# Row scatters of the routing stage spread over three steps instead of one

## The chip, the cores and the metric

The kernel runs on one core of one Trainium2 chip. The metric is the device time in microseconds (us) of one execution. A core has a matrix engine (TensorE, PE in the rows, with its weight loads as PEld), a vector engine (VectorE, DVE), an activation engine (ScalarE, ACT), GpSimd (POOL) and a sync engine (SyncE, SP) whose queue issues most of the transfers. Each engine works through its own instructions in order and waits on semaphores that the others raise. Indirect transfers, in which a list of row numbers says where each row goes, are issued by POOL.

## The reference

Three layers run after one another on 3072 tokens of 384 values (4 batches of 768 steps, 8 heads of 48):

```python
# attention: a gated linear recurrence
state = alpha[:, :, t, :, None] * state + einsum('bhd,bhe->bhde', k[:, :, t], v[:, :, t])
y[:, :, t] = einsum('bhd,bhde->bhe', q[:, :, t], state)
# layer 1: each token goes to the best of 8 experts, and is scaled by its probability
expert_idx = argmax(logits, axis=1)          # logits = normed x @ normed emb / tau
out[mask] = gate_w[mask, None] * (maximum(x[mask] @ w1[e], 0) @ w2[e])
# layer 2: all 4 experts for each token, weighted
out += p[:, e:e+1] * (maximum(x @ w1[e], 0) @ w2[e])
```

## The kernel before, in words

The tokens are cut into 24 units of 128. The first stage (about the first 170 us) is a loop over steps `i` of 0 to 28, a software pipeline written out by hand: `S1(i)` multiplies q and k of unit `i` (PE, line 480) and masks the product (DVE, 485), `S2(i-1)` forms the unit's output and the new state (PE, 516, 525, 537; the state update on DVE at 549 and 550), and `S3(i-2)` turns the output to rows of tokens (PE, 558) and copies them into a row buffer `xb` (ACT, 570). The scans that prepare a group of three units (`prep1`) stand on DVE (434, 446) and two multiplications each (`prep2`) on POOL (459, 460). The weights of layer 1 are split into a high and a low part by ACT (74) and POOL (75), one unit of weights in every second step from step 6 (`split_w`).

Units are routed in groups, `ends = [6, 12, 18, 20, 22, 24]`. When the last unit of a group is through `S3`, `route_a`, `rank`, `route_b` and `route_c` choose the expert, the place and the gate value in the next steps. In step `u1 + 4` (`u1` is the group's end) ACT scales all rows of the group (line 645) and POOL scatters them to DRAM, one indirect DMA of 128 rows of 1536 bytes a unit (line 653). The rows go to the tensor `xs`, sorted by expert. After the step of the third group's scatter, `early_load` (line 666, SP) reads the first 224 rows of the largest window back as `exw`. It waits for the scatters of the first 18 units. PE turns `exw` over in step 25 (686) and starts the first expert on it (702 and 724).

The order on each engine is that of the program text. `scatter(r)` stands ahead of `split_w` in its step before, and behind it after. Each of the row buffers is taken again by `S3` of the unit that comes as many units later as there are buffers, and is free when its scatter has landed.

Of the kernel before, what the change touches and what calls it, by code (L numbers as in the profile page):

```python
# [338 lines left out]
def attention_and_routing(tc, a, small, keep, xs, info_d, wst, wtile, load_w, split_w, psA, ps1):  # L339
# [4 lines left out]
    groups = list(zip([0] + ends[:-1], ends))  # L344
    with ExitStack() as ctx:
# [3 lines left out]
        ew = ctx.enter_context(tc.tile_pool(name="ew", bufs=2))  # L349
        bd = ctx.enter_context(tc.tile_pool(name="bd", bufs=5))  # L350
        wk = ctx.enter_context(tc.tile_pool(name="wk", bufs=2))
        xbp = ctx.enter_context(tc.tile_pool(name="xbp", bufs=10))

        cst = c1.tile([128, 736], F32, name="cst")
        ien = cst[0:112, 0:416].rearrange("p (a w) -> p a w", a=4)
# [45 lines left out]
        def load_in(g, pp, lo=0, hi=2311):  # L401
            if (g, pp) not in tins:
                tins[g, pp] = tin.tile([R, 775 + 1536], F32, tag="tin", name="tin")
            nc.sync.dma_start(out=tins[g, pp][:, lo:hi], in_=a["aqk"][g, pp][:, lo:hi])

        def load_v(g):
            v = vin.tile([128, 3, DM], F32, tag="v", name="v")
            nc.sync.dma_start(out=v, in_=a["v"][g])
            vins[g] = v

        def prefill(e):
            nc.sync.dma_start(
                out=xs[e * NR + LOW:e * NR + W0, :].rearrange("(p j) d -> p j d", j=4),
                in_=pre[0:(W0 - LOW) // 4, :].unsqueeze(1).to_broadcast([(W0 - LOW) // 4, 4, DM]),
            )
# [5 lines left out]
        def prep1(g, pp, c0=0, c1=3, part=2):  # L421
            al = tins[g, pp]
            if c0 == 0 and part != 1:
                mid[g, pp] = [
                    bd.tile([R, 774], F32, tag="G", name="G"), bd.tile([R, 774], F32, tag="bf", name="bf", bufs=6)
                ]
            G, bf = mid[g, pp]
            segs = list(range(2 * c0, 2 * c1, 3)) + [2 * c1]
            pieces = list(zip(segs, segs[1:]))
            if part != 1:  # L430
                nc.vector.memset(c3(dcon, CW)[:, :, 0:1], 1.0)
                for s0, s1 in pieces:
                    lo, hi = CW * s0, CW * s1
                    nc.vector.tensor_tensor_scan(  # L434
                        G[:, lo:hi][:, ::-1], al[:, lo + 1:hi + 1][:, ::-1], dcon[:, 0:hi - lo], 0.0,
                        op0=ALU.mult, op1=ALU.max,
                    )
            if part != 0:
                nc.scalar.activation(
                    out=bcall[:, g, c0:c1, 2 * pp:2 * pp + 2],  # L440
                    in_=c3(G, CW)[:, 2 * c0:2 * c1, 0:1].rearrange("p (c a) o -> p c (a o)", a=2), func=AF.Copy,
                )
                for s0, s1 in pieces:
                    lo, hi = CW * s0, CW * s1
                    nc.vector.reciprocal(c3(dcon, CW)[:, 0:s1 - s0, 0:1], c3(G, CW)[:, s0:s1, 0:1])
                    nc.vector.tensor_tensor_scan(  # L446
                        bf[:, lo:hi], al[:, lo:hi], dcon[:, 0:hi - lo], 0.0, op0=ALU.mult, op1=ALU.max
                    )
# [53 lines left out]
        def flush(q):  # L502
            while q:
                q.pop(0)()
# [68 lines left out]
        state, scat = {}, []  # L573
        last = len(groups) - 2

        def route_a(r):
            u0, u1 = groups[r]
            n, sl = u1 - u0, slice(u0, u1)
            rt = root_p(nc, mk, half, ssq[:, sl], n, 128)
            state[r] = rt, choose(nc, mk, wcon, raws(u0, u1), ohb[:, sl, :], n)  # L580
# [51 lines left out]
        def route_c(r):  # L632
            u0, u1 = groups[r]
            n = u1 - u0
            si, ex = state.pop(r)
            gt = gate(nc, mk, ex, n)
            state[r] = si, gt
# [8 lines left out]
                else:  # L646
                    nc.vector.tensor_scalar(xb, xb, gt[:, j:j + 1], None, op0=ALU.mult)

        def scatter(r):
            u0, u1 = groups[r]  # L650
            si = state.pop(r)[0]
            for j in range(u1 - u0):
                ins = nc.gpsimd.indirect_dma_start(
                    out=xs, out_offset=bass.IndirectOffsetOnAxis(ap=si[:, j:j + 1], axis=0),
                    in_=xbs.pop(u0 + j), in_offset=None, bounds_check=E1 * NR - 1, oob_is_err=False,
                )
                tc.declare_no_dep(ins.ins, group="xs", reason="rows of their own")
                tc.add_to_no_dep_group("xs", ins.ins)
                scat.append(ins)
# [118 lines left out]
        def prep_emb3():  # L778
            pe = mk("pe", 128, 4, 8)
            for p in range(4):  # L780
                nc.tensor.matmul(
                    pe[0:112, p, :], lhsT=embp[:, p].rearrange("e s d -> e (s d)")[:, 0:112],
                    rhs=ident[0:8, 0:8], is_transpose=True, start=(p == 0), stop=True, skip_group_check=True,
                )
            nc.vector.tensor_copy(ien[:, :, 96:104], pe[0:112])
# [33 lines left out]
        for i in range(NU + 5):  # L819
            for g in range(2, NG):  # L820
                if max(0, 3 * g - 8) == i:
                    load_in(g, 0)
                if max(0, 3 * g - 6) == i:
                    load_in(g, 1)
            for g in range(1, NG):
                if 3 * g - 2 == i:
                    load_v(g)
            if 0 < i <= E1:
                prefill(i - 1)
            if 5 <= i < 27 and i % 2:  # L830
                load_w(min((i - 3) // 2, NFB))

            steps = []
            for g in range(1, NG):
                for pp in range(2):
                    at = 3 * g - 4 + pp - (g > 2)
                    if g == 1 and pp == i:
                        steps.append((2, lambda g=g, pp=pp: prep1(g, pp)))
                    if g > 1 and at + 1 == i:
                        steps.append((0, lambda g=g, pp=pp: prep1(g, pp, part=1)))  # L840
                    if g > 1 and at == i:
                        steps.append((1, lambda g=g, pp=pp: prep1(g, pp, part=0)))
            steps = [f for _, f in sorted(steps, key=lambda x: x[0])]
            if steps and i > 1:
                steps.pop(0)()
            if 0 < i < NU:
                S1(i)
            if i == 1:
                prep_emb3()
            if 0 <= i - 2 < NU:  # L850
                S3(i - 2)
            for r, (u0, u1) in enumerate(groups):
                if i == u1 + 2 and r < last:
                    rank(r)
            if 0 <= i - 1 < NU:
                S2(i - 1)
            for r, (u0, u1) in enumerate(groups):
                if i == u1 + (3 if r < last else 2) and r <= last:
                    route_b(r)
                if i == u1 + 1:  # L860
                    flush(sums)
                    route_a(r)
                    if r > last:
                        early_rows()
                    if r >= last:
                        rank(r)
                    if r > last:
                        early_g1(0)
                        early_g1(1)
                        hl0 = early_relu(0)  # L870
                        early_g1(2)
                        early_g1(3)
            for f in steps:
                f()
            for g in range(1, NG):
                for pp in range(2):
                    at = 3 * g - 3 + pp - (g > 2)
                    if at == i:
                        prep2(g, pp, nc.gpsimd, nc.gpsimd)
                    if at + 1 == i:  # L880
                        prep4(g, pp)
            if i == 0:
                fill()
            if i == 2:
                prep_info()
            for r, (u0, u1) in enumerate(groups):
                if i == u1 + 1 and r > last:
                    route_b(r)
                if i == u1 + (4 if r < last else 2 if r == last else 1):
                    route_c(r)  # L890
                    scale(r)
                    if r < last:
                        scatter(r)
                    if r > last:
                        scatter(last)
                        scatter(r)
                        count(r)
                        tail(hl0)
            if 6 <= i < 22 and i % 2 == 0:
                split_w((i - 4) // 2)  # L900
            flush(late)
            flush(sums)
            if i == EARLY_U + 5:
                early_load()
# [389 lines left out]
```

## Time and profile before

| | |
|---|---|
| three timed runs, median (lowest, highest) | 1223.74 us (1221.97, 1224.63) |
| the profiled execution | 1219.32 us |
| its span, first to last instruction | 1217.5 us |
| mean granted TensorE clock | 0.987 |
| PE busy | 1177.6 us, 97% of the span |
| DVE, ACT, POOL busy | 393.9, 326.5, 306.8 us |

The times below are in us from the start of the span. In the page's table of 40 slices PE falls below 9 tenths at its start, in the sixth slice (about 152 to 183 us) and at its end.

### The profile page before, as it was taken

The page shows a single profiled execution, that of the slowest core. Times are in us where ns is not written, and L with a number is a line of the kernel's source. Part 1 is how long each engine was busy: PE and PEld are TensorE (multiplying, and loading weights), DVE is VectorE, ACT ScalarE, POOL GpSimd, SP SyncE. Part 2 cuts the span into 40 slices and gives each one's busy share as a digit, 9 for nine tenths or more (in the row PEclk, how much of TensorE's full clock was granted, in tenths as well). Part 3 has the DMA queues.
Part 4 walks back from the last instruction along what each step waited for, and adds up shares of the span by engine and source line. Part 5 has one row for each costly group of instructions (what it writes and reads, how often), then busy time and mean ns, then how long its engine had stood idle before and what let it go on. Part 6 is the DMA issues. An engine that isn't in the chain of part 4 may idle for free.

```text
span 1217.5 us, 17436 instructions
## 1 busy us (share of the span) xinstructions
PE 1177.6 (97%) x7219; PEld 1078.6 (89%) x7219; DVE 393.9 (32%) x823; ACT 326.5 (27%) x640; POOL 306.8 (25%) x221
## 2 busy tenths in 40 slices
PE   5999979999999999999999999999999999999996
PEld 4788879999999999999999999999999999999996
DVE  8989553222222222222212222222222122222221
ACT  3466534444444311111311111221111131111111
POOL 3567543766666300000400000130000030111111
PEclk9999989999999999999999999999999999999998
DMA  9995125544443300000300000120000010000000
GB/s 236 298 278 174 54 100 172 155 141 140 133 123 121 81 1 1 1 1 1 90 15 1 1 1 1 30 75 1 1 1 1 1 40 1 27 27 26 26 27 29
DMA packets 30032, 79.98 MB, mean 66 GB/s; under 512 B 7352, under 2 KB 11064, under 8 KB 28376
## 3 DMA queue, kind: packets, MB, share of 16 engines
q1 hardware_dynamic: 26104, 69.25, 19.5%
q0 software_dynamic: 3840, 9.54, 2.2%
q8 instruction: 58, 0.95, 0.3%
q14 instruction: 30, 0.25, 0.1%
HBM read 65.21 MB, written 13.57 MB: 65 GB/s over the span
## 4 chain that ended last, share of the span: by engine, by line
PE 87%; DVE 4%; issue 3%; ACT 0%; POOL 0%; DVEq 0%; POOLq 0%; ACTq 0%
PE h L135 14%; PE h L137 13%; PE h L136 13%; PE p L303 11%; PE p L302 11%; PE p L301 10%; PE o L234 3%; PE o L235 3%; PE o L233 3%; PE fin L558 1%; PE y L516 1%; PE A L480 1%; DVE bf L446 1%; DVE G L434 1%; DVE At L485 1%
## 5 line engine op out<-in xcount | busy, mean ns | idle before, releaser
L127 DVE SCALAR_TENSOR_TENSOR hl<-h,hh 128x512 fp32r<-128x512 f32 (+9 forms) x264 | 169.9, 644 | 733.4 <-ACT hh L126 719.0
L126 ACT ACTIVATE hh<-h 128x512 fp32r<-128x512 f32 (+9 forms) x264 | 148.2, 562 | 727.1 <-PE h L137 725.3
L75 POOL TENSOR_TENSOR wu<-wraw,wu 128x768 fp32r<-128x768 f32 x96 | 176.6, 1841 | 643.9 <-ACT wu L74 643.7
L303 PE MATMUL p<-wu,hl 128*128 128x384 f32 x768 | 258.8, 337 | 0.0
L302 PE MATMUL p<-wu,hh 128*128 128x384 f32 x768 | 258.2, 336 | 0.0
L301 PE MATMUL p<-wu,hh 128*128 128x384 f32 x768 | 258.0, 336 | 0.0
L135 PE MATMUL h<-x,wu 128*128 128x512 f32 (+1 forms) x600 | 233.0, 388 | 0.0
L137 PE MATMUL h<-x,wu 128*128 128x512 f32 (+1 forms) x600 | 230.6, 384 | 0.0
L136 PE MATMUL h<-x,wu 128*128 128x512 f32 (+1 forms) x600 | 227.9, 380 | 0.0
L302 PEld LDWEIGHTS p<-wu,hh 128*128 128x128 f32 x768 | 144.3, 188 | 7.4
L301 PEld LDWEIGHTS p<-wu,hh 128*128 128x128 f32 x768 | 144.4, 188 | 7.1
L303 PEld LDWEIGHTS p<-wu,hl 128*128 128x128 f32 x768 | 144.3, 188 | 0.0
L137 PEld LDWEIGHTS h<-x,wu 128*128 128x128 f32 x600 | 112.6, 188 | 26.6
L136 PEld LDWEIGHTS h<-x,wu 128*128 128x128 f32 x600 | 112.8, 188 | 16.1
L135 PEld LDWEIGHTS h<-x,wu 128*128 128x128 f32 x600 | 112.8, 188 | 14.5
L74 ACT ACTIVATE wu<-wraw 128x768 fp32r<-128x768 f32 x96 | 80.4, 840 | 39.6 <-PE p L303 34.1
L314 POOL DMA_INDIRECT out_dram<-acc,toki x24 | 23.4, 975 | 183.4 <-DVE acc L310 178.5
L135 PE MATMUL h<-xh,wu 128*128 128x224 f32 (+7 forms) x192 | 67.4, 351 | 0.3 <-DVE xl L198 0.3
L234 PE MATMUL o<-hl,wu 128*128 128x224 f32 (+7 forms) x192 | 65.6, 341 | 0.1
L233 PE MATMUL o<-hh,wu 128*128 128x224 f32 (+7 forms) x192 | 65.6, 342 | 0.0
L136 PE MATMUL h<-xh,wu 128*128 128x224 f32 (+7 forms) x192 | 65.5, 341 | 0.0
L137 PE MATMUL h<-xl,wu 128*128 128x224 f32 (+7 forms) x192 | 65.5, 341 | 0.0
(164 smaller groups left out, 1086.2 us busy)
## 6 DMA issues: line engine op xcount, KB each, us to landing
wraw<-in_wu_dram SPq DMA_DIRECT2D x96, 384.0 KB, 3.1
tin<-in_aqk_dram SPq DMA_DIRECT2D x14, 1011.1 KB, 11.4
xw<-xs SPq DMA_DIRECT2D x7, 672.0 KB, 6.6
v<-in_v_dram SPq DMA_DIRECT2D x8, 576.0 KB, 10.3
xs<-pre SPq DMA_DIRECT2D x8, 480.0 KB, 11.0
tin<-in_aqk_dram SPq DMA_DIRECT2D x2, 448.0 KB
tin<-in_aqk_dram SPq DMA_DIRECT2D x2, 225.8 KB, 4.4
tin<-in_aqk_dram SPq DMA_DIRECT2D x2, 224.0 KB
```

The costliest lines, as they stand in the source:

```text
L74: nc.scalar.activation(out=t[:, 0], in_=r, func=AF.Copy)
L75: nc.gpsimd.tensor_tensor(out=t[:, 1], in0=r, in1=t[:, 0].bitcast(F32), op=ALU.subtract)
L126: nc.scalar.activation(out=hh[:, 0:n], in_=ps, func=AF.Relu)
L127: nc.vector.scalar_tensor_tensor(out=hl[:, 0:n], in0=ps, scalar=0.0, in1=hh[:, 0:n].bitcast(F32), op0=ALU.max, op1=ALU.subtract)
L135: nc.tensor.matmul(ps, lhsT=w[:, 0, ks], rhs=xh(k), start=(k == 0), stop=False)
L136: nc.tensor.matmul(ps, lhsT=w[:, 1, ks], rhs=xh(k), start=False, stop=False)
L137: nc.tensor.matmul(ps, lhsT=w[:, 0, ks], rhs=xl(k), start=False, stop=(k == KD - 1))
L233: nc.tensor.matmul(o, lhsT=w[:, 0, ds], rhs=hh[:, 0:n], start=(f == 0), stop=False)
L234: nc.tensor.matmul(o, lhsT=w[:, 0, ds], rhs=hl[:, 0:n], start=False, stop=False)
L301: nc.tensor.matmul(o, lhsT=hh[:, js], rhs=w[:, 0, DM:2 * DM], start=(f == 0), stop=False)
L302: nc.tensor.matmul(o, lhsT=hh[:, js], rhs=w[:, 1, DM:2 * DM], start=False, stop=False)
L303: nc.tensor.matmul(o, lhsT=hl[:, js], rhs=w[:, 0, DM:2 * DM], start=False, stop=(f == NFB - 1))
```

## The change

The six scatters of the first and of the second group are issued two in each of three steps (`u1 + 4`, `u1 + 5`, `u1 + 6`), those of the third group three in each of two steps (22 and 23), all behind `split_w`. The fourth to sixth group are as before. The row buffers are 12 instead of 10. No transfer is added or left out.

```diff
-        xbp = ctx.enter_context(tc.tile_pool(name="xbp", bufs=10))
+        xbp = ctx.enter_context(tc.tile_pool(name="xbp", bufs=12))
...
-        def scatter(r):
+        def scatter(r, js=None):
             u0, u1 = groups[r]
-            si = state.pop(r)[0]
-            for j in range(u1 - u0):
+            si = state[r][0]
+            for j in js or range(u1 - u0):
...
-                    if r < last:
+                    if r == last - 1:
                         scatter(r)
...
             if 6 <= i < 22 and i % 2 == 0:
                 split_w((i - 4) // 2)
+
+            for r, (u0, u1) in enumerate(groups[:last - 1]):
+                n = 2 if r < 2 else 3
+                k = i - u1 - 4
+                if 0 <= k * n < u1 - u0:
+                    scatter(r, range(k * n, k * n + n))
```

POOL's instructions in steps 9 to 12, round the scatters of the first group (`xs<-xb,si` is a scatter, `wu<-wraw,wu` the split of weights, `bf` and `G` are `prep2`):

```order
 L459 TENSOR_TENSOR bf<-tin,bf 112x6x128
 L460 TENSOR_TENSOR G<-tin,G 112x6x128
-L653 DMA xs<-xb,si 24576x384 x6
 L75 TENSOR_TENSOR wu<-wraw,wu 128x768
+L653 DMA xs<-xb,si 24576x384 x2
 L459 TENSOR_TENSOR bf<-tin,bf 112x6x128
 L460 TENSOR_TENSOR G<-tin,G 112x6x128
+L653 DMA xs<-xb,si 24576x384 x2
 L459 TENSOR_TENSOR bf<-tin,bf 112x6x128
 L460 TENSOR_TENSOR G<-tin,G 112x6x128
 L75 TENSOR_TENSOR wu<-wraw,wu 128x768
+L653 DMA xs<-xb,si 24576x384 x2
```

The six stand now in three pairs, the first behind the split of weights of its step, and between the pairs stand the `prep2` of the next two steps. The second group moves in the same way in steps 16 to 18.

POOL's instructions in steps 20 to 25, round the third to sixth group (`sq_r<-ssq,half`, line 982 before and 988 after, is the root that opens a group's routing):

```order
 L75 TENSOR_TENSOR wu<-wraw,wu 128x768
-L982 TENSOR_TENSOR sq_r<-ssq,half 128x2
-L653 DMA xs<-xb,si 24576x384 x6
-L982 TENSOR_TENSOR sq_r<-ssq,half 128x2
-L653 DMA xs<-xb,si 24576x384 x2
-L982 TENSOR_TENSOR sq_r<-ssq,half 128x2
+L988 TENSOR_TENSOR sq_r<-ssq,half 128x2
+L653 DMA xs<-xb,si 24576x384 x3
+L988 TENSOR_TENSOR sq_r<-ssq,half 128x2
+L653 DMA xs<-xb,si 24576x384 x5
+L988 TENSOR_TENSOR sq_r<-ssq,half 128x2
 L653 DMA xs<-xb,si 24576x384 x4
```

The fifth group's root stands now between the third and the fourth scatter of the third group. The five behind it are the other three of the third group and the two of the fourth.

## Rows read from the trace of the kernel before

**Rows 1.** The page's chain that ended last, shares by engine.

```profile
PE 87%; DVE 4%; issue 3%; ACT 0%; POOL 0%; DVEq 0%; POOLq 0%; ACTq 0%
```

**Rows 2.** Busy us of PE, PEld, DVE, ACT, POOL in two stretches; clock, DMA share, GB/s.

```profile
90.00:120.00 30.00, 28.79 (x368) 25.11 (x367) 28.42 (x73) 19.88 (x51) 21.22 (x15) 0.90 0.59 182
...
190.00:1217.50 1027.50, 1015.90 (x5344) 937.43 (x5344) 246.40 (x412) 235.48 (x399) 206.17 (x135) 1.00 0.14 42
```

**Rows 3.** POOL's timeline, first and last scatter of three sixes: start, length, engine, instruction.

```profile
81.36 1.21 POOL L653 DMA_INDIRECT xs<-xb,si  x1 [4.73 <-ACT xb L645]
...
87.98 0.97 POOL L653 DMA_INDIRECT xs<-xb,si  x1 [0.30 <-issue]
...
117.05 1.06 POOL L653 DMA_INDIRECT xs<-xb,si  x1 [5.70 <-ACT xb L645]
...
123.53 0.98 POOL L653 DMA_INDIRECT xs<-xb,si  x1 [0.30 <-issue]
...
151.92 1.06 POOL L653 DMA_INDIRECT xs<-xb,si  x1 [7.31 <-ACT xb L645]
...
158.40 0.98 POOL L653 DMA_INDIRECT xs<-xb,si  x1 [0.30 <-issue]
159.39 0.74 POOL L982 TENSOR_TENSOR sq_r<-ssq,half 128x2 f32<-128x2 f32 x1
```

**Rows 4.** DVE's timeline at the first and second six; idle time before and releaser in brackets.

```profile
84.76 1.81 DVE L434 TENSOR_TENSOR_SCAN G<-tin,dcon 112x387 f32<-112x387 f32 x2
90.05 0.37 DVE L549 TENSOR_TENSOR U<-U,S 112x192 f32<-112x192 f32 x1 [3.48 <-PE fin L558]
...
125.73 0.37 DVE L549 TENSOR_TENSOR U<-U,S 112x192 f32<-112x192 f32 x1 [3.47 <-PE A L480]
```

**Rows 5.** PE's timeline: the state product of step 11, first products of steps 18, 19, 21, 22.

```profile
84.09 0.67 PE L537 MATMUL U<-v,kn_s 128*64 128x48 f32 x16
...
121.94 0.49 PE L480 MATMUL A<-bf,G 48*128 48x128 f32 x4
...
130.98 1.16 PE L480 MATMUL A<-bf,G 48*128 48x128 f32 x16
...
140.48 1.16 PE L480 MATMUL A<-bf,G 48*128 48x128 f32 x16
...
145.62 1.16 PE L480 MATMUL A<-bf,G 48*128 48x128 f32 x16
```

**Rows 6.** Timelines of PE, ACT and SP at the third six; DMA view's landing of exw.

```profile
154.19 1.08 PE L525 MATMUL y<-bf,S 48*48 48x128 f32 x16
...
160.56 0.60 ACT L529 ACTIVATE yt<-y 112x512 f32<-112x512 f32 x1 [5.47 <-PE U L537]
...
161.19 0.33 SPq L666 DMA_DIRECT2D exw<-xs  x1
...
exw<-xs SPq DMA_DIRECT2D x1, 336.0 KB, 3.1
...
167.76 0.74 PE L686 MATMUL ext<-ti,exw 112*128 112x112 f32 x6
```

**Rows 7.** A pair's second scatter, ACT beside it; busy us round four scatters of the output.

```profile
172.39 0.97 POOL L653 DMA_INDIRECT xs<-xb,si  x1 [0.30 <-issue]
...
173.58 0.55 ACT L710 ACTIVATE eh<-eh 128x448 fp32r<-128x448 f32 x1 [3.62 <-PE eh L702]
...
1041.00:1047.50 6.50, 6.50 (x34) 5.72 (x32) 2.13 (x4) 0.76 (x2) 3.91 (x4) 1.00 0.35 124
```

**Rows 8.** Timelines of ACT and POOL: weight splits and prep2 that the scatters move past.

```profile
83.50 0.83 ACT L74 ACTIVATE wu<-wraw 128x768 fp32r<-128x768 f32 x1
...
88.97 1.83 POOL L75 TENSOR_TENSOR wu<-wraw,wu 128x768 fp32r<-128x768 f32 x1
90.73 1.69 POOL L459 TENSOR_TENSOR bf<-tin,bf 112x768 f32<-112x768 f32 x1
...
119.19 0.83 ACT L74 ACTIVATE wu<-wraw 128x768 fp32r<-128x768 f32 x1
```

## The prediction

> **What bounds the kernel now.** I read first the page's chain that ended last: PE holds 87% of it, DVE 4%, and 3% is "issue", time in which an engine waited for nothing that the profile shows [rows 1]. Then the busy times by stretch. From 190 us on PE is busy 1015.9 of 1027.5 us: the expert stages are bound by PE, and the change doesn't touch them [rows 2]. What it can win lies before 190 us. There, between 90 and 120 us, DVE is busy 28.42 of 30 us (its scans), PE 28.79 with many short products, and the granted clock is 0.90. Both are nearly full, so whatever stops either of them is paid.
>
> Third, the timelines round the scatters. POOL issues six in a row three times: 81.36 to 88.95, 117.05 to 124.51, 151.92 to 159.38, one every 1.27 us (0.97 and a gap of 0.30) [rows 3]. In the later part of each six PE's results stop coming through. The state product of step 11 ends at 84.09 + 0.67 = 84.76, and DVE is free at 84.76 + 1.81 = 86.57, yet the state update that reads it starts at 90.05, after 3.48 us idle; in the second six the same update waits 3.47 us, until 125.73 [rows 4, 5]. In the third, ACT copies at 160.56 what PE's records end at 155.27, after 5.47 us idle [rows 6]. The name in the bracket is only PE's latest record. What is to be seen is the end of each hold: 1.10, 1.22 and 1.18 us behind the end of the sixth scatter [rows 3, 4, 6]. Its beginning: what was held had ended at 84.76 and 155.27, just behind the start of the third scatter (three times 1.27 us before the sixth: 84.2 and 154.6). So my reading is that from the third scatter in a row on PE's completions are held until some 1.1 us after the last one.
>
> A pair does not do that. The second of a pair runs from 172.39 to 173.36, and ACT takes a product of PE at 173.58, 0.9 us before such a hold would have ended [rows 7]. PE is not slowed by four output scatters either (6.50 of 6.50 us busy), but there it issues 34 products in 6.5 us, where the first stage has 368 in 30 [rows 2, 7].
>
> **The change part by part.** The transfers stay: 24 scatters, the same bytes. Only their places in POOL's order move.
>
> *First group.* With pairs the hold should be gone. DVE has work on both sides of the 3.48 us, so I take them whole: **-3.5 us**.
>
> *Second group.* Here DVE's scans end soon after, and PE sets the pace. Step 18's first product starts at 121.94, that of step 19 at 130.98: 9.04 us. An undisturbed step takes 145.62 - 140.48 = 5.14 us [rows 5]. The difference is **-3.9 us** (with part of it PE at the lower clock after the stop). The idle time of DVE alone, 3.47, is the lower bound of this term if pairs are free.
>
> *Third group.* Six scatters become three and three, with the fifth group's root of 0.74 us between them [rows 3]. A three may still hold PE from its third scatter on, about 2 us, twice. But what sets the end here is then another transfer: the reading back of `exw` waits for the sixth scatter. That one started at 158.40. In the new order the third scatter ends at 154.57 + 0.97 = 155.54, the root at 156.28, and the next three start 0.30 later at 156.58, 157.85 and 159.12: the sixth is 0.7 us later. SP issued the read 161.19 - 158.40 = 2.79 us behind the sixth, and it landed 3.1 us after that [rows 6]. New: 161.9 and 165.0. PE began to turn `exw` over at 167.76, late because of the hold. So 167.76 - 165.0 = **-2.7 us** is what can be won; the rest of the held 5.3 us becomes a wait for this read. If each three holds PE as a six does, nothing is won and the 0.7 us are lost: the bounds are -2.7 and +0.7.
>
> *POOL's order* is costed at nothing, and this is its cover. The first pair stands now behind the split of weights, which needs ACT's half, and ACT makes that after the scaling: 83.50 + 0.83 = 84.33 instead of a first scatter at 81.36. Then the split to 86.2 (1.83), pair to 88.7, two multiplications of `prep2` to 92.0 (some 1.65 each), pair to 94.6, two more to 97.9, split, pair to 102.3 [rows 8]. Before, six scatters stood ahead of the split, which began at 88.97. In the second group the split waits for ACT's at 119.19 + 0.83 - 3.5 = 116.5 (shifted by the first gain), and the same sum gives the last `prep2` at 130.0. PE needs it for step 21, at 140.48 - 7.4 = 133.1 [rows 5, 8]. The cover is 3.1 us; without it each us that POOL is late would be one of PE's. Step 16's `S3` would need the row buffer of unit 4 with ten buffers, about when its scatter lands; with twelve it is needed two steps later, so that buffers cost nothing.
>
> Sum: 3.5 + 3.9 + 2.7 = 10.1 us. The profiled execution took 1219.32 us, so the sum gives 1209.2 for one like it. It lay 4.4 us under the median of the timed runs, 1223.74, and under the lowest of them, 1221.97. Against the median I predict **1213.6 us**.
>
> **A rule that speaks against it.** The rows show PE stopped while POOL only issues transfers, three times, each ending with POOL's six [rows 3, 4, 6]. The Trainium skill, "SBUF — State Buffer", section "SBUF: two separate sides", states that engine ports and transfer ports cannot contend, that of the engines only DVE and GpSimd share a port pair, and that PE never waits on anyone there. By that rule a scatter has no way to stop PE in SBUF, the holds would have some other cause, and the time would stay at 1223.7. The trace doesn't tell the way in which the scatters act, only that the holds coincide with them; so the rule is the third rival below.
>
> **The rivals.**
>
> *Pairs still hold, but shorter.* If each pair costs PE 0.6 us, six of them take back 3.6 of the 7.4 us, and the threes leave about 1.3 of the 2.7: -5.1, 1218.6 us. For it: all pairs seen so far ran beside slower streams of products (the clock was at its lower level round 172 us), so none was tested at the rate of the first stage. Against: the 173.58 above.
>
> *Slower: a hold is paid for each burst, not for its length.* Say it begins with the second scatter of any burst. Then a pair holds PE for 0.97 + 1.1 = 2.1 us, six pairs 12.6 us, where the two sixes cost 7.4. The threes hold 1.27 + 0.97 + 1.1 = 3.3 us each, 6.7 where the six cost 5.3. Together +5.2 and +1.4, 1230 us. It decides from 1.2 us a pair on (7.4 / 6). For it: the tail of 1.1 us behind each six is as long as a scatter and might come with every burst. Against: the same ACT row, and what was held started behind the third.
>
> *Nothing changes.* The holds come from something else in these steps (the scaling of six rows on ACT, the routing chain), or they stay as long as six scatters are in six steps' reach. 1223.7 us. For it: the rule, and that four output scatters leave PE full [rows 7]. Against: three ends within 0.12 us of each other behind POOL's last scatter.
>
> **How the numbers follow.** I give the forecast 0.46 (its own range 1209 to 1218: the bounds of the third term and of the second, and the half width of the three timed runs, 1.3 us), shorter holds 0.18, no change 0.18, slower 0.18. A measurement of this kernel tells about 0.2%, 2.4 us. Faster than that: 0.46 + 0.18 = 0.64; within: 0.18; slower: 0.18. The range runs from 1208 to 1227: under it lies 0.04 (a better clock than I count), over it the larger part of the slower case, 0.13.
>
> **What would show it.** Right: PE's "issue" gaps are gone in steps 11 to 19, and DVE's state update (line 549) has no wait over 1 us there; step 19's first product starts some 7 us earlier than 130.98; `exw` is issued some 7 us earlier than 161.19, and PE waits for it in step 25. Wrong, toward slower: gaps of 2 us behind each pair, six of them, or PE waiting for `prep2` in step 21. Wrong, toward no change: DVE idle for some 3.5 us at the same places though POOL runs something else there. The weakest step is the third scatter as the place where a hold begins: it rests on three cases.

## The result and the profile after

The changed kernel takes 1214.88 us (median of 20 runs), the kernel before, on the same chip, 1224.16 us (20 runs). The ratio is 0.9917, 95% interval 0.9903 to 0.9932: 9.3 us are gone by the medians, 10.2 by the ratio, and 1213.6 was predicted. That is the result for one chip. On another the same change gave nothing, which the prediction had not thought of; the experiments come to that.

The profiled execution took 1213.84 us, with a span of 1212.1. Busy times by stretch, of the kernel after (us of the stretch, then PE, PEld, DVE, ACT and POOL, granted clock, DMA share, GB/s), answer to [rows 2]:

```profile
90.00:120.00 30.00, 28.06 (x382) 24.31 (x378) 28.45 (x70) 19.84 (x51) 24.11 (x17) 0.94 0.60 191
150.00:190.00 40.00, 35.39 (x261) 33.14 (x261) 20.84 (x95) 12.46 (x33) 13.52 (x13) 0.79 0.45 138
```

PE and DVE are as full as before between 90 and 120 us; they only get through the stage sooner. Five rows of PE before, which the readings below need, are the first products of steps 11, 12, 13 and 23 and of the expert stage (`xt`):

```profile
79.31 1.75 PE L480 MATMUL A<-bf,G 48*128 48x128 f32 x16 [0.44 <-DVE At L485]
84.69 1.48 PE L480 MATMUL A<-bf,G 48*128 48x128 f32 x15
93.86 1.75 PE L480 MATMUL A<-bf,G 48*128 48x128 f32 x16 [0.28 <-DVE At L485]
151.01 1.16 PE L480 MATMUL A<-bf,G 48*128 48x128 f32 x16
188.68 0.55 PE L192 MATMUL xt<-ti,xw 112*128 112x112 f32 x4
```

Behind `xt` nothing has moved but the start: from its first product to the end of the span it is 1217.5 - 188.68 = 1028.8 us before and 1212.1 - 183.24 = 1028.9 after. So all that the profiled executions differ by lies ahead of it.

Next, the timeline at the first and the second group (start, length, engine, instruction), which answers to [rows 3 to 5]. Its PE rows of line 480 are the first products of steps 11, 12, 13, 18 and 19:

```profile
80.61 1.75 PE L480 MATMUL A<-bf,G 48*128 48x128 f32 x16
85.99 1.18 PE L480 MATMUL A<-bf,G 48*128 48x128 f32 x16
87.71 1.21 POOL L653 DMA_INDIRECT xs<-xb,si  x1 [0.18 <-issue]
87.78 0.34 DVE L549 TENSOR_TENSOR U<-U,S 112x192 f32<-112x192 f32 x1
91.56 1.75 PE L480 MATMUL A<-bf,G 48*128 48x128 f32 x16 [0.95 <-DVE At L485]
...
119.92 1.16 PE L480 MATMUL A<-bf,G 48*128 48x128 f32 x16
120.07 1.06 POOL L653 DMA_INDIRECT xs<-xb,si  x1 [0.18 <-issue]
120.16 0.34 DVE L549 TENSOR_TENSOR U<-U,S 112x192 f32<-112x192 f32 x1
121.02 0.61 PE L492 MATMUL kn<-ti,G 112*128 112x112 f32 x4
121.44 0.98 POOL L653 DMA_INDIRECT xs<-xb,si  x1 [0.30 <-DVE dcon L445]
122.89 0.55 ACT L497 ACTIVATE kn_s<-kn 128x448 f32<-128x448 f32 x1 [2.40 <-PE fin L558]
124.47 1.22 PE L480 MATMUL A<-bf,G 48*128 48x128 f32 x16
```

The state updates of DVE (line 549) have no bracket: the waits of 3.48 and 3.47 us are gone. Step 18 to step 19 is 124.47 - 119.92 = 4.55 us, where it was 9.04 [rows 5]. A trace of the hold (the stretch in which PE's finished results reach the other engines late) is left beside a pair: `kn` ends at 121.63, ACT copies it only at 122.89. DVE has other work then, and PE doesn't wait for it.

The third group, three and three, with the tail behind it, answers to [rows 3, 6]:

```profile
144.84 1.16 PE L480 MATMUL A<-bf,G 48*128 48x128 f32 x16
145.75 1.04 POOL L653 DMA_INDIRECT xs<-xb,si  x1 [6.13 <-ACT xb L645]
148.38 0.98 POOL L653 DMA_INDIRECT xs<-xb,si  x1 [0.30 <-ACT lt L563]
149.36 0.76 POOL L988 TENSOR_TENSOR sq_r<-ssq,half 128x2 f32<-128x2 f32 x1
152.44 0.60 ACT L529 ACTIVATE yt<-y 112x512 f32<-112x512 f32 x1 [3.52 <-PE rkb L592]
152.93 0.97 POOL L653 DMA_INDIRECT xs<-xb,si  x1 [0.30 <-issue]
153.09 2.04 PE L558 MATMUL fin<-cst,yt 112*128 112x104 f32 x8 [1.27 <-issue]
154.71 0.37 DVE L549 TENSOR_TENSOR U<-U,S 112x192 f32<-112x192 f32 x1 [3.36 <-remote]
155.72 0.33 SPq L666 DMA_DIRECT2D exw<-xs  x1
161.43 1.33 PE L686 MATMUL ext<-ti,exw 112*128 112x112 f32 x6
183.24 0.55 PE L192 MATMUL xt<-ti,xw 112*128 112x112 f32 x4
```

Here the hold is still there: ACT waits 3.52 us and DVE 3.36 for what PE has done. `fin` takes 2.04 us, where it takes 1.05 to 1.14 at the full clock: the granted clock is 0.50 from 153 to 162 us, the lower of its two levels. From step 23's first product to `xt` the mean granted clock is 0.78, where it was 0.86 before. From that product to the turning over of `exw` it is 161.43 - 144.84 = 16.59 us, before 167.76 - 151.01 = 16.75. The third group won nothing.

### The profile page after: what moved, and what is told of

Same layout as the page of the kernel before. It is cut to its first block, busy times and chain, and to the rows that moved or that the text cites. A ratio compares the mean times of both kernels' runs of the same rounds, so it can differ in the third digit from the quotient of the medians.

```text
span 1212.1 us, 17429 instructions
## 1 busy us (share of the span) xinstructions
PE 1178.3 (97%) x7219; PEld 1080.6 (89%) x7219; DVE 393.9 (33%) x823; ACT 326.6 (27%) x640; POOL 307.1 (25%) x221
## 4 chain that ended last, share of the span: by engine, by line
PE 86%; DVE 5%; issue 3%; POOL 0%; ACT 0%; DVEq 0%; POOLq 0%; ACTq 0%
PE h L135 14%; PE h L137 13%; PE h L136 13%; PE p L303 11%; PE p L302 11%; PE p L301 11%; PE o L234 3%; PE o L235 3%; PE o L233 3%; DVE bf L446 1%; DVE At L485 1%; PE fin L558 1%; PE y L516 1%; DVE G L434 1%; PE A L480 1%
## 5 line engine op out<-in xcount | busy, mean ns | idle before, releaser
L135 PEld LDWEIGHTS h<-x,wu 128*128 128x128 f32 x600 | 112.8, 188 | 14.5
```

What stands on the lines that cost most here:

```text
L135: nc.tensor.matmul(ps, lhsT=w[:, 0, ks], rhs=xh(k), start=(k == 0), stop=False)
```

## The experiments

The theory (H): while POOL issues scatters back to back, PE's results are held. Rivals: the twelve buffers (B), and the other order on POOL, the split of weights and `prep2` ahead of the scatters (O). The runs come from four chips, and these were not alike, so the kernel before was timed beside each. The last column says which of the three holds the profile shows:

| kernel | chip | median us (runs) | before us | ratio to before, 95% | hold |
|---|---|---|---|---|---|
| 12 buffers alone | 3 | 1224.93 (12) | 1225.39 | 0.9998 (0.9980 to 1.0017) | all three |
| first group alone | 3 | 1222.79 (12) | 1225.39 | 0.9980 (0.9959 to 1.0000) | 2nd, 3rd |
| second group alone | 3 | 1219.80 (12) | 1225.39 | 0.9967 (0.9950 to 0.9985) | 1st, 3rd |
| third group alone | 3 | 1223.94 (12) | 1225.39 | 0.9988 (0.9969 to 1.0006) | all three |
| six at the step's end | 4 | 1213.72 (12) | 1211.10 | 1.0026 (1.0011 to 1.0040) | none |
| threes in all groups | 4 | 1212.29 (12) | 1211.10 | 1.0013 (0.9998 to 1.0027) | none |
| spacers in the third | 4 | 1215.82 (11) | 1211.10 | 1.0040 (1.0027 to 1.0054) | none |
| four small scatters more | 4 | 1212.39 (1) | 1211.10 | | none |
| before, unchanged | 0 | 1212.44 (1) | 1212.09 | | none |
| after, unchanged | 0 | 1211.46 (12) | 1212.09 | 0.9992 (0.9974 to 1.0009) | none |
| six at the step's end | 0 | 1215.78 (12) | 1212.09 | 1.0023 (1.0002 to 1.0045) | none |
| first six at end, four small | 7 | 1213.79 (12) | 1210.89 | 1.0023 (1.0005 to 1.0040) | none |

Which chip the result comes from is not known; its kernel before (1224.16) and its holds are like those of chip 3. Each of the four chips was used on one occasion only, so below "the chip" can as well mean the occasion.

**Buffers alone.**

```diff
-        xbp = ctx.enter_context(tc.tile_pool(name="xbp", bufs=10))
+        xbp = ctx.enter_context(tc.tile_pool(name="xbp", bufs=12))
```

> The kernel before with 12 row buffers instead of 10, the six scatters at once where they stood. Theory H (PE's completions are held while GpSimd issues scatters back to back, from the third on): 0, ratio 0.999 to 1.001, all three holds stay (DVE line 549 waits about 3.5 us twice). Rival B (the row buffers set the pace of prep2 or of the weighted sums): up to -9 us, the whole gain.

0.9998, and the holds stay. B has fallen on this chip.

**One group at a time.** The change, with the other groups' scatters left where they were:

```diff
-                    if r == last - 1:
+                    if r < last and r != 0:
                         scatter(r)
...
+                if r != 0:
+                    continue
                 n = 2 if r < 2 else 3
```

(0 for the first group; 1 and 2 in the two kernels beside it.)

> Only the first group's scatters are spread in pairs behind the split of weights; the second and third stay six at once ahead of it; 12 buffers. Theory H: -3.5 us (ratio 0.997); the wait of line 549 near 90 us is gone, the one near 122 us stays at 3.4 us. Rival O (what counts is that the split of weights and prep2 go ahead of the scatters on GpSimd): a gain of a third of 9.3, about -3.1, which the time can't tell from H; the run is here for its share in the sum.

> Only the second group's scatters are spread. Theory H: -4 us (ratio 0.9965), as step 18 to 19 falls from 9.04 to about 4.6 us between first products; the hold near 86 to 90 us stays. Rival (gains are not additive, since PE at the lower clock after a stop makes up or loses part of it): under -2.5 or over -5.5 us.

> Only the third group's scatters are spread, three and three in two steps. Prediction's own term: -2.7 us. Theory after the profile of the change (two shorter holds of some 2 us each, and PE at its lower clock behind them, eat it up): between -1 and +1.5 us, ratio 0.999 to 1.001. If the sum of the three single groups is far from the -9.3 us of the whole change, the steps are not independent.

At the first and the second group the hold goes where the six are spread, and stays where they are not. DVE's state updates at the first and the second group, of the kernel with the first group alone spread:

```profile
84.60 0.34 DVE L549 TENSOR_TENSOR U<-U,S 112x192 f32<-112x192 f32 x1
...
120.61 0.37 DVE L549 TENSOR_TENSOR U<-U,S 112x192 f32<-112x192 f32 x1 [3.55 <-PE A L480]
```

and of the kernel with the second alone:

```profile
92.55 0.37 DVE L549 TENSOR_TENSOR U<-U,S 112x192 f32<-112x192 f32 x1 [3.58 <-PE kn L492]
...
124.68 0.34 DVE L549 TENSOR_TENSOR U<-U,S 112x192 f32<-112x192 f32 x1
```

In time the groups give 2.0, 3.3 and 1.2 parts in a thousand of 1225.39, that is 2.5, 4.0 and 1.5 us, together 8.0; the whole change gives 10.2 by its ratio. Each single one is uncertain by some 2.3 us, so they add up as well as can be told. For the third alone the interval holds both the predicted 2.7 us and nothing. Its timeline shows why it can't be much:

```profile
152.48 1.16 PE L480 MATMUL A<-bf,G 48*128 48x128 f32 x16
156.03 0.97 POOL L653 DMA_INDIRECT xs<-xb,si  x1 [0.30 <-ACT lt L563]
160.10 0.60 ACT L529 ACTIVATE yt<-y 112x512 f32<-112x512 f32 x1 [3.56 <-PE rkb L592]
160.55 0.97 POOL L653 DMA_INDIRECT xs<-xb,si  x1 [0.30 <-issue]
162.35 0.37 DVE L549 TENSOR_TENSOR U<-U,S 112x192 f32<-112x192 f32 x1 [3.36 <-PE fin L558]
189.53 0.55 PE L192 MATMUL xt<-ti,xw 112*128 112x112 f32 x4
```

The second row is the last scatter of the first three, ended at 157.00. The results come at 160.10, in the middle of the second three, and again at 162.35, 0.83 us behind its last. Two threes with one root of some 0.75 us between them hold PE nearly as one six. The stage itself tells more than the times. From step 23's first product to `xt` it is 189.53 - 152.48 = 37.05 us here, 38.40 in the whole change, and 37.58 to 37.85 in the four kernels that leave the third six together (before, twelve buffers, first alone, second alone). The third group is worth less than a microsecond, either way.

**Six at the end of the step, threes, spacers, small rows.** These were to tell spreading from order, and to find what a hold needs. In the first, `n = 6` in the changed loop; in the second, `n = 3`; the third is

```diff
...
+                if r < 2 and 0 <= k < 3:
+                    scatter(r, range(2 * k, 2 * k + 2))
+                if r == 2 and k == 0:
+                    for j in range(0, 6, 2):
+                        if j:
+                            nc.gpsimd.tensor_tensor(out=fw, in0=fw, in1=fw, op=ALU.add)
+                        scatter(r, range(j, j + 2))
```

(`fw` is a scratch tile), and the fourth adds, at the end of step 21, four scatters of 32-byte rows:

```diff
+            if i == 21:
+                for j in range(4):
+                    ins = nc.gpsimd.indirect_dma_start(
+                        out=keep["spare"], out_offset=bass.IndirectOffsetOnAxis(ap=state[2][0][:, j:j + 1], axis=0),
+                        in_=inf[:, j, :], in_offset=None, bounds_check=E1 * NR - 1, oob_is_err=False,
+                    )
...
```

> The changed kernel, but each group's six scatters again at once, at the end of the step, behind the split of weights; 12 buffers. It moves GpSimd's order as the change does and takes away the spreading. Theory H (holds behind the third scatter in a row): the holds come back some 5 to 10 us later than before, and the time is that of before within 2.5 us or, as prep2 is behind six scatters, up to 3 us slower: 1222 to 1227. Rival O (the order on GpSimd gives the gain): 1214 to 1217, no hold that ends 1.1 us behind the sixth scatter.

> The changed kernel with three scatters in each of two steps for all three groups. Theory H with a hold from the third scatter on: each three holds PE for some 2 us, of which DVE and PE hide a part; 1215.5 to 1220, that is 0.5 to 5 us over the changed kernel. Rival D (a hold needs four or more in a row, or the third group's stop in the changed kernel is the routing's): as the changed kernel within 1 us, 1214 to 1216, no wait of line 549 above 1 us.

> The changed kernel, but the third group's six scatters are all issued at the end of step 22, as three pairs with an addition on a scratch tile of 128 x 768 (some 1.5 us of GpSimd) between two pairs. The output does not depend on the scratch tile. Theory H: no hold in steps 23 to 25, the first product of step 25 and the fin of step 25 come 2 to 4 us sooner, and 1 to 4 us of the time are won against the changed kernel (1211 to 1214) unless the reading back of exw, issued behind the sixth scatter, becomes the last. Rival (third group's stop comes from the scaling and routing of these steps, or any scatter counts): no change against the changed kernel.

> The changed kernel with four more scatters in a row at the end of step 21, rows of 32 bytes into a tensor that nothing reads, with the third group's indices; the output is unchanged. Step 21 to 22 has no scatter in the changed kernel, so a hold there is due to these. Theory H1 (it is GpSimd's issuing that holds PE, whatever the bytes): a wait of 1.5 to 3 us shows on DVE or ACT for PE's results, ending about 1.1 us behind the fourth. Theory H2 (the rows' bytes hold it): no wait over 0.8 us there.

They ran on chip 4, where the kernel before itself takes 1211.10 us, 14 less than on chip 3. No hold is in any of the four, not behind six scatters in a row either. So what a hold needs could not be seen: there was none, and a time like that of before tells neither for H nor for O. What the runs do show is the price of the edits without holds: by their medians the three timed ones are 1 to 5 us slower than before (for the threes the interval reaches no change).

**The kernel before and the change on one chip.** The open question was now whether the hold belongs to the chip (C) or to the place in the kernel (P):

> The kernel before, unchanged, for its profile beside the next two. Two theories, since six scatters at the end of a step (the run of that name) showed no hold on a second chip, where the kernel before takes 1211.1 us and not 1225. Theory C (the chip): the hold belongs to the first chip. On the second the kernel before shows no stretch of over 3 us without a completion of PE between 80 and 162 us, and about 1211 us; on the first the three holds of 4 to 7.5 us as before. Theory P (the place): what stands around the six scatters makes the hold, so that it shows in this kernel on either chip, and the 14 us between the chips are something else.

> The changed kernel, unchanged, against the kernel before on the chip of this call. Theory C: on the first chip again about 0.992; on the second no gain, ratio 0.999 to 1.003, since there is no hold to take away and the pairs only shift GpSimd's other work. Theory P: 0.990 to 0.994 on either chip.

> The six scatters of each group at once at the end of the step, as in the run of that name. Theory C: on the first chip the holds are there (stretches of 4 to 7.5 us without a completion of PE, ending about 1.1 us behind the sixth scatter) and the time is that of before, ratio 0.998 to 1.004; on the second as measured there, 1.0026. Theory P: no holds on either chip, and on the first chip a gain of some 8 us, ratio about 0.993.

These three ran on chip 0. The unchanged kernel before, first and second six there, timeline of POOL, DVE and PE:

```profile
87.65 0.97 POOL L653 DMA_INDIRECT xs<-xb,si  x1 [0.31 <-ACT xb L570]
88.69 0.34 DVE L549 TENSOR_TENSOR U<-U,S 112x192 f32<-112x192 f32 x1
88.93 0.97 POOL L653 DMA_INDIRECT xs<-xb,si  x1 [0.30 <-issue]
...
121.61 1.17 PE L480 MATMUL A<-bf,G 48*128 48x128 f32 x16
122.21 0.97 POOL L653 DMA_INDIRECT xs<-xb,si  x1 [0.30 <-ACT sj L569]
123.40 0.34 DVE L549 TENSOR_TENSOR U<-U,S 112x192 f32<-112x192 f32 x1
123.48 0.97 POOL L653 DMA_INDIRECT xs<-xb,si  x1 [0.30 <-issue]
127.19 1.75 PE L480 MATMUL A<-bf,G 48*128 48x128 f32 x16 [0.95 <-DVE At L485]
```

It is the same code with the same six scatters 1.27 us apart, and DVE's update runs between the fourth and the fifth without a wait. Step 18 to 19 takes 5.58 us, not 9.04 [rows 5]. The hold goes with the chip; the place alone does not make it. And the change itself is worth nothing there: 0.9992, interval 0.9974 to 1.0009.

On chip 3 the ten row buffers cost nothing that was seen; on chip 0 they show. Behind the same first six ACT waits for a buffer whose scatter hasn't landed:

```profile
92.85 0.49 ACT L570 ACTIVATE xb<-fin 128x384 f32<-128x384 f32 x1 [2.65 <-DMA xs<-xb,si]
```

No kernel with twelve buffers shows this wait on chips 0, 4 and 7. The change, which has twelve, was no faster for it, and twelve buffers alone were not run on chip 0.

The DMA view sets the two kinds of chips apart in one more row, that of the transfers that POOL issues. First of the kernel before on the chip of the result, then of the same kernel on chip 0 (the last number is the median us to landing):

```profile
xs<-xb,si POOLq DMA_INDIRECT x24
```

```profile
xs<-xb,si POOLq DMA_INDIRECT x24, 3.0
```

In all the traces with holds, and in none without, the records of the landings are too incomplete for a median: the whole trace of before has 3163 of them, that of the same kernel on chip 0 has 3560. Whether one cause lies behind the missing records and the held results, or whether the recording itself does the holding, no run here tells.

Six at the end of the step is slower on chip 0 as on chip 4, and there its profile shows why, without a hold in it. Step 16, timeline of that kernel on chip 0:

```profile
98.07 0.43 SPq L64 DMA_DIRECT2D wraw<-in_wu_dram  x1
105.33 1.16 PE L480 MATMUL A<-bf,G 48*128 48x128 f32 x16
108.01 0.84 ACT L74 ACTIVATE wu<-wraw 128x768 fp32r<-128x768 f32 x1 [7.70 <-DMA wraw<-in_wu_dram]
108.86 0.52 ACT L497 ACTIVATE kn_s<-kn 128x448 f32<-128x448 f32 x1
109.44 0.61 PE L492 MATMUL kn<-ti,G 112*128 112x112 f32 x4 [2.94 <-ACT kn_s L497]
117.31 1.16 PE L480 MATMUL A<-bf,G 48*128 48x128 f32 x16
```

ACT stands 7.70 us before a split whose weights haven't landed (the load of the first row, which landed 9.9 us after its issue), and behind it in ACT's order is the copy that PE needs; PE waits 2.94 us and step 16 takes 11.98 us. In the change itself, on the same chip, that load was issued 3.7 us sooner:

```profile
94.33 0.43 SPq L64 DMA_DIRECT2D wraw<-in_wu_dram  x1
```

and ACT waited 0.67 us for it. Not all of the step is lost in the end: from step 11's first product to `xt` it is 104.39 us, with pairs 101.88. The waits of SP's queue between 80 and 105 us say where it began. Of the six at the end, and then of the change itself, on chip 0 (us in total, times, longest):

```profile
SPq L404 <- POOL G L460: 7.9, 2, 6.5
```

```profile
SPq L404 <- POOL G L460: 1.7, 2, 1.3
```

With six scatters between the split and `prep2`, the buffer of `tin` comes free later (line 404 loads it), and SP's loads, the weights among them, queue behind it. Pairs leave `prep2` between them.

**First six at the end, and four small scatters, once more.** The last run joined the two open questions:

```diff
-                n = 2 if r < 2 else 3
+                n = (6, 2, 3)[r]
```

with the four small scatters of above.

> The changed kernel with the first group's six scatters at once at the end of the step (behind the split of weights) and four added scatters of 32-byte rows into a tensor that nothing reads at the end of step 21; the output is unchanged. On a chip with holds (the kernel before at about 1225 us): theory S (spreading is what helps) has a hold of 3 to 7 us at the first group's six and a time 3 to 6 us above that of the changed kernel there; theory O (the order on GpSimd helps) has none and 1214 to 1216. Whether four rows of 32 bytes hold PE is open: over 2 us without a completion that ends about 1 us behind the fourth, if issuing and completions count; under 1 us, if the bytes count. On a chip without holds (before at about 1212 us): no such stretch at either place, ratio 1.000 to 1.004.

It ran on chip 7, which showed no hold behind either burst: 1.0023. Both questions stay open.

## Why the prediction came out, and where it did not hold

**The first and the second group.** The terms were -3.5 and -3.9. Step 12 to 13 went from 9.17 us (84.69 to 93.86 before) to 91.56 - 85.99 = 5.57, which is -3.6; step 18 to 19 went from 9.04 to 4.55, which is -4.5. From step 11's first product to step 23's it is 64.23 us after (80.61 to 144.84) and 71.70 before (79.31 to 151.01), -7.5 against the -7.4 of the two terms. The two single runs, -2.5 and -4.0, agree within what they can tell.

**The third group** is the term that failed: -2.7 was taken, of the bounds -2.7 and +0.7. The time behind the sixth scatter was right to the hundredth (`exw` issued at 152.93 + 2.79 = 155.72), but PE did not wait for it. Each three held PE, as the bound of +0.7 had it, and the products behind the stop ran at the lower clock. At line 686 0.2 us were won, and the stretch from there to the expert stage's first product `xt` (line 192) took 183.24 - 161.43 = 21.81 us, before 188.68 - 167.76 = 20.92. So the term is about +0.7 in this profile; in the profile of that group alone it is about -0.6 (37.05 us where those with a six have 37.58 to 37.85), and by the times of that run between -3.8 and +0.7. The granted clock goes with it: 0.78 in this one from step 23 to `xt`, 0.86 in the other, as before. The wait for `exw` that was forecast does exist where nothing holds PE: 0.51 us for the changed kernel on chip 0, and with spacers 4.06 on chip 4.

**The sum** was 10.1 us, and 9.3 by the medians (10.2 by the ratio) were measured. In the profiles it is less, 1219.32 to 1213.84; the profiled execution of before lay 4.8 us under its kernel's median, as the prediction had allowed for, while that of after lay only 1.0 under. The terms in their stages leave 7.5 - 0.7 = 6.8 us; less the 1.3 by which step 11 started later after (80.61, before 79.31) that is 5.5, the 5.48 between the two profiled executions. The rest of the 9.3 lies between executions, and no term accounts for it. So that the sum came within 1 us of the measured gain is in part luck: 2.7 us of it were not won, and some 2.5 us that no term names stand in their place.

**POOL's order at nothing** held for the change. But the cover named for it, `prep2` ahead of step 21, is not what comes first when the cover goes. It is SP's queue behind `prep2`, the weights' load, and ACT, as the six at the end showed (+2.8 us).

**The third scatter as the place where a hold begins** was called the weakest step, and it is not sharp. Beside pairs results came late as well, by 1.26 us at 121.63, in slack. "Pairs still hold, but shorter" was thus right as to what happens at this pair, and wrong as to its price, since DVE and PE were busy meanwhile. Holds paid per burst in full, the slower rival, have fallen.

**What the prediction took for granted** was that what the trace of before shows belongs to the kernel. The holds were read rightly, and they belong to this kernel on some chips. The Trainium skill, "SBUF — State Buffer", section "SBUF: two separate sides", states that PE never waits on anyone there. On chip 0 the rows agree with it (no wait at 88.69 and 123.40), and the traces from chips 4 and 7 show no such wait either; beside the same six scatters on chip 3 PE's results come some 3.5 us late, in whatever way. On chip 0 the third rival, nothing changes, is the result. Whether six at the end would be held on chip 3, so that spreading and not order is what helps there, was not run. Order brought no gain on chips 0 and 4, and the third six of before, with no split or `prep2` behind it, is held too [rows 6]; that speaks for spreading and is no proof.

## What to carry to other kernels

A stall in one trace that no dependence explains, such as an engine's finished results arriving late, should be looked for in a trace of the same kernel on another chip before a change is built on it. When a burst of issues is moved or cut up, follow what stands behind it on the queue of its engine to the loads that wait for that engine's work: here that was the difference, where nothing was held, between pairs (0.9992) and six at once (1.0023) in the same place. Cutting a burst in half is not spreading it: where holds were seen, two threes with some 0.75 us of other work between them held PE nearly as long as a six.

## What was not expected of the hardware

The kernel before took 1224.16 and 1225.39 us in two series of runs, and 1210.89 to 1212.09 on three other chips, with the same code. The three holds, of which DVE shows 3.48 and 3.47 us and ACT 5.47 [rows 4, 6], add up to 12.4 us, near the 12 to 14.5 us between them, but waits are not their price. From step 11's first product to `xt` the profile of before has 109.37 us and that of the same kernel on chip 0 has 100.34: 9.0 us, and behind `xt` both have 1028.8. The holds go with landings of POOL's transfers that are missing from the records. For this kernel the chip mattered more than the change.
